# Three edits to the order of work in a fused attention and gated-MLP kernel: joined attention insertions, one accumulator bank for two products, and weight sums at seven in five steps

## The chip, the cores and the metric

The kernel runs on one core of a Trainium2 chip. The metric is the device time of one execution in microseconds (us). PE is the matmul engine (TensorE), DVE the vector engine, ACT the scalar engine, POOL the GpSimd engine, and SP issues the DMAs from one queue, in order.

## The reference

```python
scores = scale * np.matmul(q_c, k_c.transpose(0, 1, 2, 4, 3))      # chunks of 64 tokens, head_dim 64, 64 heads in all
attn = softmax(scores)                                             # over the 64 keys of the chunk
x = (attn @ v_c)  -> (4608 tokens, 512)
gate = 1.0 / (1.0 + np.exp(-(x @ w_gate)))                         # w_gate, w_val: 512 x 1536
out = gate * (x @ w_val) @ w_out                                   # w_out: 1536 x 512
```

Everything is float32; the MLP products are made of three products of float32r halves (high x high, low x high, high x low).

## The kernel before

The 4608 tokens are nine blocks of 512 (`m` = 0 to 8), the hidden layer is twelve tiles of 128 (`f`). Attention is cut into 36 units, four to a block; a unit is one `products` (scores, L163, eight small matmuls), a softmax on DVE and ACT, a turn of the probabilities on DVE (`spread`, L554, sixteen 32x32-block transposes), and one `values` (product with v, L224, eight small matmuls, whose result ACT copies out of PSUM).

Blocks 0 to 2 are done plainly: a step `hidden` (L267) makes one hidden tile with 24 matmuls of 128x512 and `down` (L281) adds it to four output accumulators with 12. Blocks 3 to 8 are done as three pairs (`n` = 0 to 2). In a pair, an item is two hidden tiles of one weight (`p` of six, `which` = gate or value; 12 items), and its four 512-token results come from seven products instead of eight (a Strassen-Winograd scheme); each `product` (L416) is six matmuls of 128x512. The operands that the scheme needs are sums of weight quarters and of x quarters. Products are numbered 1 to 7. Product 1 accumulates in bank `x`, 6 in `y`, 2 on top of 1 in `x`, 7 and 4 on top in `y`, 5 in a third bank `z` (`sole`, L426), 3 on top in `z`. DVE reads `y` and `z` between them: u2 after 6 (L439), u3 after 7 (L458), c22 after 5 (L460), c21 after 4 (L475), c12 after 3 (L478). Per item `i` the program runs `first(i)` (products 1, 6), `last(i-1)` (4, 3) and `middle(i)` (5, 7, 2). Bank `z` alternates between `g0` and `g1`, by `which`. After the items a pair runs 24 `outward` steps (L494), the second weight matrix.

The attention of later blocks is woven in by a generator, `flow` (L506). It yields small DVE costs that `tick` (L573) releases by a credit (`SHARES`, L45), and two letters for PE work that `insert` (L587) releases at set places: "S" for the scores of two units, "A" for the values of two units. In the pairs the two letters come at different places. PE and DVE keep the program's order here; `manual_schedule` says so.

The weight sums are made once, on POOL, while blocks 1 and 2 run: `keep(2)` (L661) asks for two of 24 `keep_sums` (L331) after each step from block 1, `f` = 2. One `keep_sums` is two adds into `a_val`, four into `a_sum`, a cast and a subtract into `a_both`, and one DMA to DRAM. `a_val` and `a_sum` share the two-buffer ring `ob` with the output tiles of `evacuate` (L294, PSUM copy at L305 or L307, DMA at L308); `a_both` has one buffer. `load_group` (L360) loads given weights and sums again for each item.

Of the kernel before, what the change touches and what calls it, by code (L numbers as in the profile page):

```python
# [8 lines left out]
F32 = mybir.dt.float32  # L9
# [3 lines left out]
ALU = mybir.AluOpType  # L13
AX = mybir.AxisListType

P = 128
D = 64
NB = 9
TB = 512
# [22 lines left out]
FIRST_PAIR = 3  # L42


SHARES = {1: 2.5, 2: 2.8, "up": 1.05, "down": 1.3}  # L45


@with_exitstack
def chunk_attn_moe(ctx: ExitStack, tc: tile.TileContext, q, k, v, w, out):


    nc = tc.nc
# [7 lines left out]
    ps_g = ctx.enter_context(tc.tile_pool(name="ps_g", bufs=2, space=bass.MemoryType.PSUM))  # L60
# [94 lines left out]
    def load_values(j):  # L155
        m, h, u = units[j]
        vt = ap2.tile([P, 2, 4, D], F32, name="vt")
        nc.sync.dma_start(vt, v[2 * m + h, u].rearrange("p (a c d) -> p a c d", a=2, c=4))
        state[j]["vt"] = vt

    def products(j):  # L163
        s = state[j]
        sc = ps_a.tile([P, 512], F32, tag="psa", name="sc")
        for a in range(2):
            for t in range(2):
                for c in ((0, 1), (1, 0))[a * t]:
                    n0 = (2 * t + c) * D
                    nc.tensor.matmul(  # L170
                        sc[c * D:(c + 1) * D, (2 * a + t) * P:(2 * a + t + 1) * P],
                        lhsT=s["qt"][:, a, n0:n0 + D], rhs=s["kb"][:, a, :, n0:n0 + D],
                        start=True, stop=True,
                    )
        return sc.rearrange("p (g k) -> p g k", k=D)
# [182 lines left out]
    groups, wo, xc, hid = {}, {}, {}, {}  # L358
# [55 lines left out]
    banks = {}  # L414

    def product(n, p, which, r, bank, start, stop):  # L416
        lhs, name = groups[n, p, which][r]
        x, k = xc[n, name], 0
        for c in range(2):
            for wpart, part in ((0, 0), (0, 1), (1, 0)):  # L420
                nc.tensor.matmul(  # L421
                    bank, lhsT=lhs(wpart, c), rhs=x[:, part, c], start=start and k == 0, stop=stop and k == 5,
                    skip_group_check=True)
                k += 1

    def sole(n, p, which):  # L426
        z = ps_g.tile([P, TB], F32, tag=f"g{which}", name="cz", bufs=1)
        product(n, p, which, 5, z, True, True)
        return z

# [11 lines left out]
    def gated(n, f, b, value):  # L442

        h = hid[n, f][:, b]
        nc.vector.tensor_tensor(out=h, in0=value, in1=h, op=ALU.mult)

    def middle(n, p, which):
        x, y, s1, u2 = banks[n, p, which]
        f = 2 * p
        if which == 0:  # L450
            for i in range(2):
                hid[n, f + i] = wp.tile([P, 2, TB], F32, tag=f"o{f + i}", name="hid")
        z = banks.pop((n, "z"), None) or sole(n, p, which)
        if (p, which) == (0, 0):
            product(n, p, which, 2, x, False, True)
        product(n, p, which, 7, y, False, True)
        u3 = mp.tile([P, TB], F32, tag="ob", name="u3")
        nc.vector.tensor_tensor(out=u3, in0=y, in1=s1, op=ALU.add)  # L458
        c22 = hid[n, f + 1][:, 1] if which == 0 else u3
        nc.vector.tensor_tensor(out=c22, in0=z, in1=u3, op=ALU.add)  # L460
        if (p, which) != (0, 0):
            product(n, p, which, 2, x, False, True)
        if which == 0:
            nc.scalar.activation(hid[n, f][:, 0], x, AF.Sigmoid)
        else:
            gated(n, f + 1, 1, u3)
            gated(n, f, 0, x)
        banks[n, p, which] = y, z, s1, u2

    def last(n, p, which):  # L470
        y, z, s1, u2 = banks.pop((n, p, which))
        f = 2 * p
        product(n, p, which, 4, y, False, True)
        c21 = hid[n, f + 1][:, 0] if which == 0 else s1
        nc.vector.tensor_tensor(out=c21, in0=y, in1=s1, op=ALU.add)  # L475
        product(n, p, which, 3, z, False, True)
        c12 = hid[n, f][:, 1] if which == 0 else u2
        nc.vector.tensor_tensor(out=c12, in0=z, in1=u2, op=ALU.add)  # L478
        if which == 0:
            nc.scalar.activation(hid[n, f + 1], hid[n, f + 1], AF.Sigmoid)  # L480
            nc.scalar.activation(hid[n, f][:, 1], hid[n, f][:, 1], AF.Sigmoid)
        else:
            gated(n, f + 1, 0, s1)
            gated(n, f, 1, u2)

    def split(n, f, b):
        h = hid[n, f][:, b]
# [18 lines left out]
    def flow():  # L506


        kept = None
        for j in range(8, 4 * NB + 2, 2):  # L510
            more = j < 4 * NB
            if more:
                yield "S"
                scv = [products(j), products(j + 1)]
                if j + 2 < 4 * NB:
                    load(j + 2), load(j + 3)
                if kept:
                    yield from spread(*kept, range(12, 16))
                pr = ap2.tile([P, 2, 8, D], F32, name="pr", bufs=1)
                for i in range(2):  # L520
                    yield 1.4
                    mx = sm.tile([P, 8], F32, name="mx")
                    nc.vector.reduce_max(out=mx, in_=scv[i], axis=AX.X)
                    nc.vector.tensor_tensor(
                        out=pr[:, i], in0=scv[i], in1=mx.unsqueeze(2).broadcast_to([P, 8, D]), op=ALU.subtract)
                pr = pr.rearrange("p u g k -> p (u g) k")
                nc.scalar.activation(pr, pr, AF.Exp, scale=0.125)
            elif kept:
                yield from spread(*kept, range(12, 16))
            if kept:  # L530
                yield "A"
                values(j - 2), values(j - 1)
                if more:
                    load_values(j), load_values(j + 1)
            else:
                yield "wait"
            n, rest = divmod(j - 4 * FIRST_PAIR, 8)
            if n > 0 and rest == 0:
                yield ("open", n - 1)
                yield from operands(n - 1)  # L540
            if not more:
                return
            yield 1.5
            sums = sm.tile([P, 16], F32, name="sums2", bufs=1)
            nc.vector.reduce_sum(out=sums, in_=pr, axis=AX.X)
            nc.vector.tensor_scalar_add(out=sums, in0=sums, scalar1=1e-9)
            inv = sm.tile([P, 16], F32, name="inv2", bufs=1)
            nc.vector.reciprocal(out=inv, in_=sums)
            yield 1.2
            nc.vector.tensor_tensor(out=pr, in0=pr, in1=inv.unsqueeze(2).broadcast_to([P, 16, D]), op=ALU.mult)  # L550
            kept = pr, pbd2
            yield from spread(*kept, range(12))
# [10 lines left out]
            nc.vector.transpose(out=pb[dst, :, c, h, i, :], in_=ps[src, h::2, k, :])  # L563

    ahead = flow()
    now = dict(item=next(ahead), credit=0.0, ticks=0, since=0, unit=8, open=-1)

    def advance():
        now["unit"] += 2 * (now["item"] == "A")
        now["item"] = next(ahead, None)  # L570
        now["since"] = now["ticks"]

# [14 lines left out]
    def insert(upto=4 * NB, pieces=0):  # L587


        if now["item"] == "S" or (  # L590
                now["item"] == "A" and now["unit"] < upto and now["ticks"] >= now["since"] + pieces):
            advance()

    def due(n):
# [39 lines left out]
        run(op)  # L634
    kept = [(p, which, c) for p in range(6) for which in range(2) for c in range(2)]

    def keep(n):
        for _ in range(n):
            if kept:
                p, which, c = kept.pop(0)  # L640
                if c == 0:
                    keep_given(p, which)
                keep_sums(p, which, c)

    def rest():
        for m in range(1, FIRST_PAIR):
            upto = 4 * (m + 2) if m == 1 else 4 * (m + 3)
            for f in range(2 if m == 1 else 0, NF):
                if m == 2 and f == 7:
                    now["open"] = 0  # L650
                step(m, f, "")
                tick(SHARES[m])
                insert(upto, 2)
                finish()
                tick(SHARES[m])
                insert(upto, 2)
                if m == 1:
                    keep_outer(f)
                    if f == 11:
                        keep_outer(0), keep_outer(1)  # L660
                keep(2)  # L661
                if m == 2:
                    if f == 8:
                        for which in range(2):
                            load_group(0, 0, which)
        for n in range(3):
            m0 = FIRST_PAIR + 2 * n
            upto = 4 * (m0 + 4)
            order = [(p, which) for p in range(6) for which in range(2)]
            due(n)  # L670
            for i, (p, which) in enumerate(order):
# [77 lines left out]
```

## Time and profile before

| | us |
|---|---|
| median of 3 runs (lowest, highest) | 956.03 (954.69, 957.15) |
| the profiled execution: its time | 960.18 |
| the profiled execution: its span | 958.4 |
| PE busy in that span | 929.6 (97%) |
| DVE, ACT, POOL busy | 601.8, 340.7, 134.1 |

PE is busy almost throughout, so what counts is where it is not, where it runs at the lower clock, and how many matmuls of which length it must issue. Idle time of the other engines costs nothing by itself. The span is from the first to the last instruction of one execution.

### The profile page before, as it was taken

The page shows a single profiled execution, that of the slowest core. Times are in us where ns is not written, and L with a number is a line of the kernel's source. Part 1 is how long each engine was busy: PE and PEld are TensorE (multiplying, and loading weights), DVE is VectorE, ACT ScalarE, POOL GpSimd, SP SyncE. Part 2 cuts the span into 40 slices and gives each one's busy share as a digit, 9 for nine tenths or more (in the row PEclk, how much of TensorE's full clock was granted, in tenths as well). Part 3 has the DMA queues.
Part 4 walks back from the last instruction along what each step waited for, and adds up shares of the span by engine and source line. Part 5 has one row for each costly group of instructions (what it writes and reads, how often), then busy time and mean ns, then how long its engine had stood idle before and what let it go on. Part 6 is the DMA issues. An engine that isn't in the chain of part 4 may idle for free.

```text
span 958.4 us, 13077 instructions
## 1 busy us (share of the span) xinstructions
PE 929.6 (97%) x4960; PEld 763.5 (80%) x4960; DVE 601.8 (63%) x999; ACT 340.7 (36%) x556; POOL 134.1 (14%) x204
## 2 busy tenths in 40 slices
PE   6999999999969999999999999999999999999998
PEld 4777888888847888788888888888888888888886
DVE  6889973676527657777677675677776635544432
ACT  5799752233214323231333432313143321112222
POOL 1000006999838000000000000000000000000000
PEclk7999999999989999999999999999999999999999
DMA  8688985444453343657666756666565655556661
GB/s 270 215 287 299 307 309 180 132 133 129 136 164 109 102 132 132 193 198 226 207 212 239 252 198 218 228 202 206 179 231 191 218 211 192 196 188 209 220 220 44
DMA packets 81279, 189.61 MB, mean 198 GB/s; under 512 B 7488, under 2 KB 38208, under 8 KB 76608
## 3 DMA queue, kind: packets, MB, share of 16 engines
q1 hardware_dynamic: 81216, 188.77, 58.9%
q8 instruction: 39, 0.64, 0.3%
q14 instruction: 24, 0.20, 0.1%
HBM read 150.99 MB, written 37.75 MB: 197 GB/s over the span
## 4 chain that ended last, share of the span: by engine, by line
PE 70%; POOL 9%; DMA 8%; DVE 5%; ACT 4%; issue 2%; SPq 1%; ACTq 0%; DVEq 0%; POOLq 0%
PE acc L499 21%; PE cy L421 15%; PE cz L421 10%; PE cx L421 10%; PE g L261 6%; PE acc L287 4%; DMA w_raw<-w_in 3%; POOL a_sum L344 3%; POOL a_both L347 3%; DMA sums<-a_both 2%; POOL a_val L338 2%; PE sc L170 2%; PE av L231 2%; POOL a_both L346 1%; DMA out<-ob 1%
## 5 line engine op out<-in xcount | busy, mean ns | idle before, releaser
L261 PE MATMUL g<-xt,w 128*128 128x512 f32 (+1 forms) x960 | 208.7, 372 | 6.0 <-ACT hf L270 1.7
L261 PEld LDWEIGHTS g<-xt,w 128*128 128x128 f32 x960 | 168.1, 189 | 41.5 <-ACT hf L270 4.0
L499 PE MATMUL acc<-wr,hh 128*128 128x512 f32 x576 | 177.7, 390 | 0.0
L421 PE MATMUL cy<-xc,wr 128*128 128x512 f32 x648 | 159.4, 389 | 0.4 <-DVE u L458 0.4
L421 PEld LDWEIGHTS cy<-xc,wr 128*128 128x128 f32 x648 | 121.6, 188 | 26.0 <-DVE u L458 0.8
L499 PEld LDWEIGHTS acc<-wr,hh 128*128 128x128 f32 x576 | 107.9, 188 | 22.7 <-ACT raw L242 0.3
L499 PE MATMUL acc<-wr,hl 128*128 128x512 f32 x288 | 112.0, 389 | 0.0
L421 PE MATMUL cz<-xc,wr 128*128 128x512 f32 x432 | 106.3, 391 | 0.0
L421 PE MATMUL cx<-xc,wr 128*128 128x512 f32 x432 | 106.2, 391 | 0.0
L563 DVE STREAM_TRANSPOSE pbd<-pr 32x256 f32<-32x256 f32 x224 | 97.7, 436 | 4.1
L491 DVE TENSOR_TENSOR hl<-hid,hh 128x512 fp32r<-128x512 f32 x72 | 49.6, 688 | 79.0 <-ACT hh L489 75.8
L421 PEld LDWEIGHTS cz<-xc,wr 128*128 128x128 f32 x432 | 80.6, 188 | 17.6 <-issue 1.2
L421 PEld LDWEIGHTS cx<-xc,wr 128*128 128x128 f32 x432 | 80.7, 188 | 17.4 <-issue 0.9
L287 PE MATMUL acc<-w,hh 128*128 128x512 f32 x288 | 90.6, 396 | 1.1 <-ACT hh L274 0.7
L489 ACT CAST hh<-hid 128x512 fp32r<-128x512 f32 x72 | 44.8, 623 | 123.7 <-PE acc L499 96.3
L287 PEld LDWEIGHTS acc<-w,hh 128*128 128x128 f32 x288 | 52.6, 188 | 13.8 <-issue 1.9
L499 PEld LDWEIGHTS acc<-wr,hl 128*128 128x128 f32 x288 | 54.1, 188 | 11.3
L272 DVE TENSOR_TENSOR hf<-g,hf 128x512 f32<-128x512 f32 (+1 forms) x40 | 25.4, 635 | 57.8 <-PE g L261 53.8
L439 DVE TENSOR_TENSOR u<-cy,s 128x512 f32<-128x512 f32 x36 | 24.8, 688 | 57.9 <-PE cy L421 57.8
L338 POOL TENSOR_TENSOR a_val<-w 128x256 f32<-128x256 f32 x48 | 37.7, 805 | 163.8 <-ACT xt L249 147.4
L458 DVE TENSOR_TENSOR u<-cy,s 128x512 f32<-128x512 f32 x36 | 24.9, 690 | 53.9 <-PE cy L421 53.8
L287 PE MATMUL acc<-w,hl 128*128 128x512 f32 x144 | 56.1, 390 | 0.0
(103 smaller groups left out, 1006.5 us busy)
## 6 DMA issues: line engine op xcount, KB each, us to landing
wr<-sums SPq DMA_DIRECT2D x72, 512.0 KB, 4.5
wr<-outer SPq DMA_DIRECT2D x36, 1024.0 KB, 4.8
w_raw<-w_in SPq DMA_DIRECT2D x36, 512.0 KB, 5.8
wr<-given SPq DMA_DIRECT2D x36, 512.0 KB, 3.6
sums<-a_both SPq DMA_DIRECT2D x24, 512.0 KB, 3.5
qt<-q_in SPq DMA_DIRECT2D x36, 256.0 KB, 4.4
kbd<-k_in SPq DMA_DIRECT2D x72, 128.0 KB, 4.4
vt<-v_in SPq DMA_DIRECT2D x36, 256.0 KB, 4.1
```

Source lines behind the costliest of these rows:

```text
L261: nc.tensor.matmul(ps[:, tok], lhsT=wt[f, which][:, wpart, c:c + P], rhs=x[:, part, i, tok], start=n == 0, stop=n == 11)
L272: nc.vector.tensor_tensor(out=hf, in0=pv, in1=hf, op=ALU.mult)
L287: nc.tensor.matmul(acc[m, t], lhsT=hx[:, ts], rhs=wt[f, 2][:, wpart], start=f == 0 and i == 0, stop=f == NF - 1 and i == 2,)
L338: nc.gpsimd.tensor_tensor(out=val[:, 2 * n:2 * n + 2], in0=parts[:, 0], in1=parts[:, 1], op=ALU.add)
L344: nc.gpsimd.tensor_tensor(out=o, in0=x, in1=y, op=op)
L347: nc.gpsimd.tensor_tensor(out=both[:, :, 1], in0=sm4, in1=both[:, :, 0].bitcast(F32), op=ALU.subtract)
L421: nc.tensor.matmul(bank, lhsT=lhs(wpart, c), rhs=x[:, part, c], start=start and k == 0, stop=stop and k == 5, skip_group_check=True)
L458: nc.vector.tensor_tensor(out=u3, in0=y, in1=s1, op=ALU.add)
L489: nc.scalar.copy(hh, h)
L491: nc.vector.tensor_tensor(out=hl, in0=h, in1=hh.bitcast(F32), op=ALU.subtract)
L499: nc.tensor.matmul(acc[m, t], lhsT=hx[:, ts], rhs=wo[f][:, wpart], start=f == 0 and i == 0, stop=f == NF - 1 and i == 2)
L563: nc.vector.transpose(out=pb[dst, :, c, h, i, :], in_=ps[src, h::2, k, :])
```

## The change

Four edits. (1) In the pairs, "A" and "S" become one letter "AS": the values of two units and then the scores of the next two are issued back to back. The first of these scores goes into bank `g1`, the second into the shared `psa` ring of two, whose two buffers the two `values` have just filled. All sixteen transposes of a unit pair now stand ahead of the insertion; before, four came after the scores. (2) Bank `z` is always `g0`, and the order inside an item's products is 3, 4 in `last` and 7, 5, 2 in `middle` (the first item of a pair excepted). (3) Credit per tick in the pairs is 1.15, not 1.05. (4) The weight sums are asked for at seven in five steps instead of ten.

```diff
-SHARES = {1: 2.5, 2: 2.8, "up": 1.05, "down": 1.3}
+SHARES = {1: 2.5, 2: 2.8, "up": 1.15, "down": 1.3}
-    def products(j):
+    def products(j, apart=False):
-        sc = ps_a.tile([P, 512], F32, tag="psa", name="sc")
+        sc = ps_g.tile([P, 512], F32, tag="g1", name="sc", bufs=1) if apart else ps_a.tile(
+            [P, 512], F32, tag="psa", name="sc")
     def sole(n, p, which):
-        z = ps_g.tile([P, TB], F32, tag=f"g{which}", name="cz", bufs=1)
+        z = ps_g.tile([P, TB], F32, tag="g0", name="cz", bufs=1)
     def middle(n, p, which):
-        z = banks.pop((n, "z"), None) or sole(n, p, which)
         if (p, which) == (0, 0):
+            z = banks.pop((n, "z"), None) or sole(n, p, which)
             product(n, p, which, 2, x, False, True)
-        product(n, p, which, 7, y, False, True)
+            product(n, p, which, 7, y, False, True)
+        else:
+            product(n, p, which, 7, y, False, True)
+            z = sole(n, p, which)
     def last(n, p, which):
+        product(n, p, which, 3, z, False, True)
+        c12 = hid[n, f][:, 1] if which == 0 else u2
+        nc.vector.tensor_tensor(out=c12, in0=z, in1=u2, op=ALU.add)
         product(n, p, which, 4, y, False, True)
...
-        product(n, p, which, 3, z, False, True)
-        c12 = hid[n, f][:, 1] if which == 0 else u2
-        nc.vector.tensor_tensor(out=c12, in0=z, in1=u2, op=ALU.add)
     def flow():
+            joined = now["joined"]
+            if more and joined:
+                yield from spread(*kept, range(12, 16))
+                yield "AS"
+                values(j - 2), values(j - 1)
+                scv = [products(j, True), products(j + 1)]
+                load_values(j), load_values(j + 1)
+            elif more:
                 yield "S"
                 scv = [products(j), products(j + 1)]
...
-    def keep(n):
-        for _ in range(n):
+    def keep(done, wanted):
+        for _ in range(wanted - done):
...
-                keep(2)
+                keep(24 - len(kept), (7 * (12 * m + f - 13)) // 5)
...
-            upto = 4 * (m0 + 4)
+            upto = 4 * NB
+            now["joined"] = True
```

SP's queue around the output tiles of block 1 (`out<-ob`), before: 20 of the 24 sums stand ahead of the output tiles, the last six of them here.

```order
L348 DMA sums_2428<-a_both 512x1x256 x2
L348 DMA sums_2537<-a_both 512x1x256
L158 DMA vt<-v_in 128x512 x2
L348 DMA sums_2537<-a_both 512x1x256
L348 DMA sums_2627<-a_both 512x1x256 x2
L149 DMA qt<-q_in 128x512
L152 DMA kbd_87<-k_in 64x2x256 x2
L149 DMA qt<-q_in 128x512
L152 DMA kbd_88<-k_in 64x2x256 x2
L158 DMA vt<-v_in 128x512 x2
L308 DMA out<-ob 128x512 x4
```

And now:

```order
L349 DMA sums_2540<-a_both 512x1x256 x2
L149 DMA qt<-q_in 128x512
L152 DMA kbd_87<-k_in 64x2x256 x2
L149 DMA qt<-q_in 128x512
L152 DMA kbd_88<-k_in 64x2x256 x2
L158 DMA vt<-v_in 128x512 x2
L149 DMA qt<-q_in 128x512
L152 DMA kbd_87<-k_in 64x2x256 x2
L149 DMA qt<-q_in 128x512
L152 DMA kbd_88<-k_in 64x2x256 x2
L158 DMA vt<-v_in 128x512 x2
L309 DMA out<-ob 128x512 x4
```

Fourteen sums now stand ahead of the output tiles and ten behind them; between the fourteenth and the output tiles SP has two sets of loads of q, k and v and no sum.

PE in the first pair, items 2 and 3 (operands: `xc_3454` is product 1's, 3504 is 6's, 3520 4's, 3463 3's, 3460 5's, 3467 7's, 3456 2's; all weights `wr`), before:

```order
L421 MATMUL cx_3822<-xc_3454,wr_3743 128x512 x6
L421 MATMUL cy_3823<-xc_3504,wr_3743 128x512 x6
L421 MATMUL cy_3750<-xc_3520,wr_3647 128x512 x6
L421 MATMUL cz_3790<-xc_3463,wr_3647 128x512 x6
L231 MATMUL av_3860<-pbd_89,vt_3438 64x128 x8
L231 MATMUL av_3871<-pbd_89,vt_3440 64x128 x8
L421 MATMUL cz_3886<-xc_3460,wr_3743 128x512 x6
L421 MATMUL cy_3823<-xc_3467,wr_3744 128x512 x6
L421 MATMUL cx_3822<-xc_3456,wr_3743 128x512 x6
```

And now, items 1 and 2:

```order
L422 MATMUL cx_3724<-xc_3454,wr_3646 128x512 x6
L422 MATMUL cy_3725<-xc_3504,wr_3646 128x512 x6
L422 MATMUL cz_3698<-xc_3463,wr_3380 128x512 x6
L422 MATMUL cy_3653<-xc_3520,wr_3380 128x512 x6
L232 MATMUL av_3761<-pbd_89,vt_3438 64x128 x8
L232 MATMUL av_3772<-pbd_89,vt_3440 64x128 x8
L171 MATMUL sc_3783<-kbd0_87,qt_3284 64x128 x8
L171 MATMUL sc_3792<-kbd1_88,qt_3288 64x128 x8
L422 MATMUL cy_3725<-xc_3467,wr_3647 128x512 x6
L422 MATMUL cz_3822<-xc_3460,wr_3646 128x512 x6
L422 MATMUL cx_3724<-xc_3456,wr_3646 128x512 x6
```

Product 3 moved ahead of 4 and product 5 behind 7, so products 4 and 7 stand between the two users of `z`; the scores, which before stood at other places in the program, now follow the values directly. Over the three pairs, seven insertions of scores and eight of values become seven joined ones and one of values.

## Rows read from the trace of the kernel before

**Rows 1.** Waits of PE in the whole span: us in total, times, longest us.

```profile
PE sc L170 <- DMA kbd<-k_in: 10.8, 4, 8.1
```

**Rows 2.** Windows, by stage: us, busy us of each engine, PE clock, DMA share, GB/s.

```profile
263.00:300.00 37.00, 26.04 (x125) 19.96 (x124) 16.31 (x29) 5.61 (x8) 19.47 (x29) 0.91 0.46 142
```

**Rows 3.** Timeline of PE, 258 to 300 us (start us, us, what, [idle before]).

```profile
263.49 5.60 PE L261 MATMUL g<-xt,w 128*128 128x512 f32 x24
277.19 1.97 PE L170 MATMUL sc<-kbd,qt 128*64 128x128 f32 x16 [8.10 <-DMA kbd<-k_in]
292.95 0.62 PE L287 MATMUL acc<-w,hh 128*128 128x512 f32 x2
```

**Rows 4.** Timeline of SP's queue, 258 to 284 us.

```profile
258.30 12.81 SPq L348 DMA_DIRECT2D sums<-a_both  x3
271.83 1.65 SPq L152 DMA_DIRECT2D kbd<-k_in  x2
276.53 7.59 SPq L308 DMA_DIRECT2D out<-ob  x4
```

**Rows 5.** Timeline of DVE and ACT, 255 to 300 us: output tiles of block 1.

```profile
267.25 0.69 DVE L307 COPY ob<-acc 128x512 f32<-128x512 f32 x1 [5.70 <-POOL a_sum L344]
270.60 0.58 ACT L305 COPY ob<-acc 128x512 f32<-128x512 f32 x1 [9.25 <-POOL a_both L347]
282.55 0.69 DVE L307 COPY ob<-acc 128x512 f32<-128x512 f32 x1 [14.62 <-DMA out<-ob]
```

**Rows 6.** Timeline of POOL: first, fourteenth and twentieth weight sum.

```profile
152.05 1.45 POOL L338 TENSOR_TENSOR a_val<-w 128x256 f32<-128x256 f32 x2 [147.36 <-ACT xt L249]
233.75 1.29 POOL L347 TENSOR_TENSOR a_both<-a_sum,a_both 128x512 fp32r<-128x512 f32 x1
269.31 1.26 POOL L347 TENSOR_TENSOR a_both<-a_sum,a_both 128x512 fp32r<-128x512 f32 x1
```

**Rows 7.** Chain that ended last, 143 to 156 us: output tiles of block 0.

```profile
146.47 3.23 DMA out<-ob
```

**Rows 8.** Timeline of PE around one insertion, first pair, 440 to 447 us.

```profile
440.80 1.52 PE L421 MATMUL cx<-xc,wr 128*128 128x512 f32 x6
442.25 1.97 PE L170 MATMUL sc<-kbd,qt 128*64 128x128 f32 x32
444.15 1.65 PE L421 MATMUL cx<-xc,wr 128*128 128x512 f32 x6
445.64 1.52 PE L421 MATMUL cy<-xc,wr 128*128 128x512 f32 x6
```

**Rows 9.** Timeline of PE and DVE, 389 to 396 us: the first pair's first items.

```profile
391.00 1.52 PE L421 MATMUL cy<-xc,wr 128*128 128x512 f32 x6
392.91 1.65 PE L421 MATMUL cy<-xc,wr 128*128 128x512 f32 x6 [0.39 <-DVE u L458]
392.89 0.69 DVE L460 TENSOR_TENSOR hid<-cz,u 128x512 f32<-128x512 f32 x1
```

**Rows 10.** Timeline of PE and ACT: values and the copies of them.

```profile
459.33 1.97 PE L231 MATMUL av<-pbd,vt 128*64 128x128 f32 x32
462.69 0.57 ACT L242 COPY raw<-av 128x512 f32<-128x512 f32 x1
546.48 0.58 ACT L242 COPY raw<-av 128x512 f32<-128x512 f32 x1 [0.16 <-PE av L231]
```

**Rows 11.** Timeline of PE and DVE, 616 to 630 us: a round with DVE behind.

```profile
620.96 2.88 PE L421 MATMUL cy<-xc,wr 128*128 128x512 f32 x12
623.68 2.88 PE L421 MATMUL cz<-xc,wr 128*128 128x512 f32 x12
625.59 0.66 DVE L478 TENSOR_TENSOR u<-cz,u 128x512 f32<-128x512 f32 x1
```

**Rows 12.** Windows, DVE's hl (L276) alone: beside POOL's sums, and after them.

```profile
155.00:255.00 100.00, 10.64 (x12) 1.00 0.40 126
310.00:378.00 68.00, 4.84 (x7) 1.00 0.39 120
```

More of the change, by code (lines that the diff above doesn't have):

```diff
@@ L482, in last @@
         else:
+            gated(n, f, 1, u2)
             gated(n, f + 1, 0, s1)
-            gated(n, f, 1, u2)
     def split(n, f, b):
@@ L511, in flow @@
             more = j < 4 * NB
-            if more:
+            joined = now["joined"]
[6 more added lines that the diff above has]
+            elif more:
                 yield "S"
                 scv = [products(j), products(j + 1)]
+            if more:
                 if j + 2 < 4 * NB:
                     load(j + 2), load(j + 3)
-                if kept:
+                if kept and not joined:
                     yield from spread(*kept, range(12, 16))
@@ L529, in flow @@
                 yield from spread(*kept, range(12, 16))
-            if kept:
+            if kept and not (more and joined):
                 yield "A"
@@ L565, in chunk_attn_moe @@
     ahead = flow()
-    now = dict(item=next(ahead), credit=0.0, ticks=0, since=0, unit=8, open=-1)
+    now = dict(credit=0.0, ticks=0, since=0, unit=8, open=-1, joined=False)
+    now["item"] = next(ahead)
     def advance():
-        now["unit"] += 2 * (now["item"] == "A")
+        now["unit"] += 2 * (now["item"] in ("A", "AS"))
         now["item"] = next(ahead, None)
@@ L590, in insert @@
         if now["item"] == "S" or (
-                now["item"] == "A" and now["unit"] < upto and now["ticks"] >= now["since"] + pieces):
+                now["item"] in ("A", "AS") and now["unit"] < upto and now["ticks"] >= now["since"] + pieces):
             advance()
```

## Prediction

> **What bounds the kernel now.** I read the table of busy times first: PE is busy for 97% of the span, so a change can win only where PE is idle or slow, or where it issues less. PE's waits then name the one large idle stretch: of all that PE waits for, the keys of a score matmul cost most, 10.8 us, of which one wait is 8.1 us [rows 1]. The windows by stage show where: in the 37 us from 263 to 300, PE is busy for 26.04 and its granted clock is 0.91 of full [rows 2]; in the stretches of the pairs it is never idle by more than a few tenths. So the third block's start is one target, and the number and the spacing of small insertions in the pairs is the other.
>
> How much the stall costs is read from PE's own order. Six matmuls of 128x512 take 1.36 us (twelve from 620.96 to 623.68) [rows 11]. An insertion of two units costs 445.64 - 440.80 - 2 x 1.36 = 2.12 us all in, of which the 32 records of its small matmuls take 1.90 and the way in and out 0.22 [rows 8]. From 263.49 PE has 24 matmuls of the up kind (5.44), one insertion of scores (2.12), twelve down (2.72) and 24 up (5.44), and should begin the next down block at 279.21. It begins it at 292.95 [rows 3]. So **13.74 us** are lost, 10.96 as idle time [rows 2], the rest because PE runs at half rate after the long wait: 16 records of scores take the 1.97 us there that 32 take elsewhere [rows 3, 8].
>
> Who causes it is read on SP and POOL. The keys that PE waits for are issued at 271.83, because SP, in order, sat on three weight sums from 258.30 for 12.81 us [rows 4]. POOL makes the first sum from 152.05 and ends the twentieth at 270.57: 5.93 us each [rows 6]. Twenty of them are asked for ahead of block 1's output tiles, in less time than POOL needs. The output copies use the same ring as the sums, so DVE's waits for POOL until 267.25 and ACT's until 270.60; the third copy, DVE's second, waits until 282.55 for an output DMA that SP could issue only at 276.53 [rows 4, 5], and what stands behind it on DVE is late too.
>
> **The change part by part.**
>
> *Weight sums, seven in five steps.* Fourteen now stand ahead of block 1's output tiles. POOL ended its fourteenth at 235.04 [rows 6], 28 us before the tiles are due at 263.5. Copies one and two then find a free ring, SP has no sum to sit on, and the keys are loaded long before 269. The 13.74 us go. What is late next is the third copy: it needs the first output DMA, issued at about 262.5, which lands 3.23 us later by block 0's row [rows 7], or 6.0 by block 1's (276.53 to 282.55) [rows 4, 5], so at 265.7 to 268.5. Its accumulator is wanted again at 263.49 + 5.44 + 2.12 + 1.36 = 272.4, so the DMA is covered; some DVE work queues behind the copy. I give back **0.3** and bound that by 0 and 3 us, half of one slow DMA. The other ten sums move beside the third block: 10 x 5.93 = 59 us of POOL from about 270 to 330, when that block ends at about 366. There SP again meets sums ahead of loads of q, k and v; I take 0, since these loads are asked for some 10 us or more ahead of their use, and bound it by a repeat of the 8.1 us wait [rows 1]. POOL's adds slow DVE: twelve `hl` took 0.887 us each beside the sums, seven took 0.691 after them [rows 12]. That is 0.2 us for each of some four more steps, on an engine off the path.
>
> *Joined insertions.* No matmul goes or comes. Seven pairs of stops become seven stops, so seven ways in and out of 0.22 us go: **1.54**. The seam between values and scores is taken as nothing, since two units follow each other inside 32 records without one; its bounds are 0 and a full 0.22, that is 0 to 1.54 in all. The second score goes into the bank of the first values, so it waits for ACT's copy of them. It is due three quarters into the insertion, 3 x 0.95 = 2.85 us after its start. Where ACT was free the copy began 0.16 us after the ACT work before it, as soon as the values were done, and took 0.58 [rows 10]: done at about 1.8. Where ACT stood behind a softmax and two sigmoids it ended at 463.26, 3.93 us after the values began at 459.33 [rows 10]: 1.08 late. In the new order ACT's instruction ahead of these copies is the copy of the next item's product 1, finished long before. I take 0 and bound it by 7 x 1.08 = 7.6.
>
> *Order 3, 4, 7, 5, 2 with one bank z.* Product 5 now overwrites the bank that DVE reads after product 3. Between them stand 4 and 7. Counted from the start of 3, it ends at 1.36, its last matmul drains by 1.52 [rows 8], DVE can add at about 1.63 and is done 0.69 later, at 2.32; product 5 is due at 3 x 1.36 = 4.08. That leaves 1.7 us for DVE to be late. In a round with DVE well behind, 3 began at 623.68 and its add at 625.59, 1.91 after it, so 0.28 late [rows 11]. So 33 rounds cost nothing. One place does cost: in the first pair DVE has a softmax between the sums, and 4, which waits only for u3, began at 392.91 instead of 391.00 + 1.36 [rows 9]. Now 3 comes first and waits for c22, done at 393.58: **0.7** more, once. The other two pairs have no softmax there. Here the Trainium skill's page Perfetto Trace Analysis (Optimizing Tensor Performance, Matmuls) speaks against the change: independent groups should rotate through PSUM banks, so that one's evacuation overlaps the next one's matmuls. By that rule every round would show its evacuation; by the row above it does not, because two products to another bank stand between.
>
> *More credit per tick* moves DVE's softmax pieces earlier and adds no work; PE covers it as before. Loads of v, q and k are now issued together at the joined stop, a round or more ahead of use; I take 0.
>
> Sum: -13.74 + 0.30 - 1.54 + 0.70 = -14.28. The profiled execution took 960.18, so its like would take 945.9. That execution is 4.15 above the median of the runs; taken from the median, **941.8**. A difference of 0.3% (2.9 us) is about what a measurement of this kernel can tell from none.
>
> **The rivals.**
> A. The stall moves. POOL restarts behind the output DMAs and SP sits on sums 15 to 24 until a load of keys or values is late in the third block. For it: SP's order has these loads behind sums. Against: POOL's pace leaves some 10 us. It gives back 8.1: 949.9.
> B. A residue at the output tiles, by DVE work queued behind the third copy, or because the profiled execution had a worse stall than the others (it is 4.15 slower than their median): 3 to 4 us back, 945 to 946.
> C. The second score waits for ACT in each joined stop: 7.6 back, 949.4. Against: ACT's order there.
> D. **Slower**: the single bank z. If DVE ends its add of 3 after product 5 is due, PE stops in 33 rounds. The gain is used up when each loses 14.28 / 33 = 0.43 us, that is when DVE begins the add 1.7 + 0.43 = 2.1 us late in every round; with no overlap at all, 0.27 + 0.69 = 0.96 per round, 32 us, 973.5. For it: DVE is the busiest engine after PE and gets its pieces in bigger lumps. Against: the worst lateness that I found is 0.28.
> The rotation rule of the Trainium skill named above is this rival's mechanism; the trace so far does not bear it out.
> E. Sums still late: the change would not do what it says if POOL were held by something else than its own pace. POOL's sums follow each other without gaps up to the twentieth, which speaks against; little would change, 955.
>
> **How the numbers follow.** Forecast 0.72, A 0.07, B 0.13, C 0.04, D 0.03, E 0.01. Faster by over 0.3%: all but D and E, 0.96; within 0.3%: 0.01; slower: 0.03. The range reaches down to the sum without the give-backs less the runs' own scatter of 1.3 (956.03 - 13.74 - 1.54 - 1.3 = 939.4, so 939.5), and up over B to 948.0.
>
> **What would show it.** In the profile after: PE's long wait for keys is gone, and the windows of the third block show PE full and a granted clock of 1.0; POOL's sums show a gap at block 1's output tiles after the fourteenth and end at about 330; output copies of block 1 wait for PE or one DMA, not for POOL. In the pairs 64 small records stand together seven times, with one way in and out of 0.22. Product 5 does not wait for DVE's c12; the first pair's product 3 waits about 1.2 us for c22. It is wrong if PE waits at product 5, at the second score of a joined stop, or for keys, values or `hl` in the third block.

## The result and the profile after

The changed kernel takes **945.29 us** (median of 5 runs, 944.48 to 945.75); the kernel before takes 956.03 (5 runs beside it, 954.69 to 958.22). The ratio is 0.9883, 95% interval 0.9867 to 0.9900: about 11 us faster. I had said 941.8 with a range of 939.5 to 948.0. The profiled execution of the changed kernel took 945.75, its span is 944.0; before, these were 960.18 and 958.4. So the profiled executions differ by 14.4 and the medians by 10.7; 960.18 lies above all five runs of the kernel before.

The page of the changed kernel, busy times and the slices of PE, POOL and PE's granted clock:

```profile
PE 926.0 (98%) x4960; PEld 763.6 (81%) x4960; DVE 602.9 (64%) x999; ACT 342.5 (36%) x556; POOL 134.1 (14%) x204
PE   6999999999999999999999999999999999999998
POOL 1000005997069700000000000000000000000000
PEclk7999999999999999999999999999999999999999
```

The single low slice in the middle of POOL's row is the pause that the new pacing makes at block 1's output tiles. Three of PE's waits over the span, where [rows 1] stood before (us in total, times, longest):

```profile
PE sc L171 <- DMA kbd<-k_in: 1.3, 2, 1.1
PE cz L422 <- DVE hid L464: 1.1, 1, 1.1
PE acc L503 <- ACT ob L306: 0.6, 1, 0.6
```

The wait of 8.1 for keys is gone (the 1.3 that are left belong to the start). Two small waits in the pairs are new. The window that answers to [rows 2] (us, busy us of PE, PEld, DVE, ACT, POOL, PE clock, DMA share, GB/s):

```profile
262.00:300.00 38.00, 38.00 (x237) 31.15 (x236) 26.34 (x45) 13.74 (x18) 30.17 (x43) 1.00 0.39 131
```

PE is never idle there and runs at full clock, where it was busy for 26.04 of 37 before. The timeline of the same stretch, all engines (start us, us, what, [idle before]), against [rows 3 to 6]:

```profile
232.58 1.30 POOL L348 TENSOR_TENSOR a_both<-a_sum,a_both 128x512 fp32r<-128x512 f32 x1
...
261.74 4.21 SPq L309 DMA_DIRECT2D out<-ob  x4
...
262.82 5.60 PE L262 MATMUL g<-xt,w 128*128 128x512 f32 x24
...
264.26 0.69 DVE L308 COPY ob<-acc 128x512 f32<-128x512 f32 x1 [2.54 <-DMA out<-ob]
...
267.16 1.97 POOL L339 TENSOR_TENSOR a_val<-w 128x256 f32<-128x256 f32 x2 [33.28 <-DMA out<-ob]
...
268.35 1.97 PE L171 MATMUL sc<-kbd,qt 128*64 128x128 f32 x32
...
278.54 0.62 PE L288 MATMUL acc<-w,hh 128*128 128x512 f32 x2
```

POOL ends its fourteenth sum at 233.88 and waits until the output tiles have left. The output DMAs go at 261.74, not 276.53; the third copy waits for one of them and is done at 264.95, 6.8 us before PE wants that bank. From the 24 matmuls to the second down block PE needs 278.54 - 262.82 = 15.72, which is what its matmuls add up to without a stall; before it needed 29.46 [rows 3].

### The profile page after: what moved, and what is told of

Its sections match the earlier page's. It is cut to its first block, busy times and chain, and to the rows that moved or that the text cites. A ratio compares the mean times of both kernels' runs of the same rounds, so it can differ in the third digit from the quotient of the medians.

```text
span 944.0 us, 13066 instructions
## 1 busy us (share of the span) xinstructions
PE 926.0 (98%) x4960; PEld 763.6 (81%) x4960; DVE 602.9 (64%) x999; ACT 342.5 (36%) x556; POOL 134.1 (14%) x204
## 4 chain that ended last, share of the span: by engine, by line
PE 83%; DVE 6%; DMA 5%; ACT 4%; issue 1%; SPq 1%; ACTq 0%; DVEq 0%
PE acc L503 20%; PE cy L422 15%; PE g L262 14%; PE cz L422 10%; PE cx L422 10%; PE acc L288 7%; DMA w_raw<-w_in 4%; PE av L232 3%; PE sc L171 3%; DVE w_raw L132 1%; DVE w L137 1%; DVE w_raw L134 1%; ACT w_raw L130 1%; DMA wr<-outer 1%; ACT w_raw L129 1%
## 5 line engine op out<-in xcount | busy, mean ns | idle before, releaser
L422 PE MATMUL cz<-xc,wr 128*128 128x512 f32 x432 | 109.8, 389 | 1.1 <-DVE hid L464 1.1
L440 DVE TENSOR_TENSOR u<-cy,s 128x512 f32<-128x512 f32 x36 | 24.9, 691 | 54.2 <-PE cy L422 54.1
L468 ACT ACTIVATE hid<-cx 128x512 f32<-128x512 f32 x18 | 10.8, 599 | 108.2 <-PE cx L422 108.2
```

The source lines that it names most:

```text
L422: nc.tensor.matmul(bank, lhsT=lhs(wpart, c), rhs=x[:, part, c], start=start and k == 0, stop=stop and k == 5, skip_group_check=True)
L440: nc.vector.tensor_tensor(out=u2, in0=y, in1=s1, op=ALU.add)
```

## Where PE's time went, in three stretches

All profiled executions were cut in the same way. A is the start of the 24 up matmuls after block 1's last down block (263.49 in [rows 3]); B is the time from there to the first pair's first product; C is the time from that product to the start of the last outward matmul. For the changed kernel B and C rest on these two rows of PE's timeline (365.30 - 262.82 = 102.48, 939.23 - 365.30 = 573.93):

```profile
365.30 1.52 PE L422 MATMUL cz<-xc,wr 128*128 128x512 f32 x6
...
939.23 0.39 PE L503 MATMUL acc<-wr,hl 128*128 128x512 f32 x1
```

| profiled execution of | A | B | C | span |
|---|---|---|---|---|
| before | 263.49 | 116.63 | 573.53 | 958.4 |
| before, another (e12) | 259.08 | 115.19 | 573.53 | 952.5 |
| changed | 262.82 | 102.48 | 573.93 | 944.0 |
| changed, another (e5) | 262.52 | 102.48 | 573.98 | 943.7 |
| e1 before + new pacing | 263.78 | 102.48 | 573.54 | 944.1 |
| e7 before + nine in five | 263.05 | 102.80 | 573.53 | 944.1 |
| e2 changed, old pacing | 262.45 | 116.14 | 573.92 | 957.4 |
| e6 before, keys from ACT | 276.00 | 102.48 | 573.53 | 956.7 |
| e3 changed, s1 first | 259.66 | 102.48 | 572.65 | 939.5 |
| e4 changed, three mends | 260.79 | 102.48 | 571.65 | 939.6 |
| e8 changed, not joined | 262.15 | 102.48 | 575.77 | 944.7 |
| e10 one product between | 260.56 | 102.48 | 579.83 | 947.6 |
| e9 5 directly behind 3 | 263.11 | 102.48 | 606.26 | 976.6 |
| e11 e4 with a fuller start | 263.45 | 102.48 | 571.63 | 942.3 |

Three things are seen at once. B is 102.48 wherever the sums are paced (102.80 in e7), and 12.7 to 14.2 more where they are not: that is the stall, and it is not the same in each execution. (In e6 the stall stands ahead of A, so A holds it.) C repeats to 0.06 where the program in it is the same, so a few tenths in the pairs can be read from one execution: the pairs became **0.40 longer**, not 0.84 shorter as my terms for them sum to. And the start, A, scatters by 4.7 us (e6 aside) between executions whose program up to there is the same or nearly so; that scatter is in the times of the runs.

## The experiments

**e1 and e2: pacing alone, and all the rest alone.** e1 is the kernel before with `keep(24 - len(kept), (7 * (12 * m + f - 13)) // 5)`; e2 is the changed kernel with

```diff
-                keep(24 - len(kept), (7 * (12 * m + f - 13)) // 5)
+                keep(24 - len(kept), 2 * (12 * m + f - 13))
```

> The kernel before with the weight sums at seven in five steps, nothing else. Theory: the pacing alone removes the stall at block 1's output tiles, and the edits in the pairs come to about nothing together (seven joined stops save 0.37 each, 2.6 in all; given back are 0.71 at the first pair's first item, 3 x 0.46 at the second outward step of each pair and 0.84 at an output tile of the first pair), net +0.3. Then this run takes 945.0, 0.3 below the changed kernel. Rival 1: the pairs gain 0.84, as the prediction's terms for them sum to; then 946.1. Rival 2: the stall cost all executions 13.74, as in the profiled one, and the pairs lose 3; then 942.3. In the trace: no wait for keys at 268, and the pairs as before.

> The changed kernel with the old pacing of the weight sums, two after each step. Theory: the stall is back, its size from one execution to the next as in the kernel before, and the median is 956.4 (before + 0.3). Rival 1 (the pairs gain 0.84): 955.2. Rival 2 (the pairs lose 3): 959. In the trace: a wait for keys of several us near 268 to 277 and copies of output tiles that wait for POOL.

e1: 944.52 against 957.92 before, ratio 0.9871 (0.9850 to 0.9892). e2: 957.99, ratio 1.0005 (0.9988 to 1.0021). So the pacing carries the whole gain, and the edits in the pairs together give nothing that the times show. The times cannot tell e1 from the changed kernel (0.9883); the stretches can: C is 573.54 and 573.92, the same 0.4 apart as between before and changed.

**e7: how few sums ahead are few enough.** Before with `9 *` in place of `7 *`.

> The kernel before with the sums at nine in five steps: 18 ahead of block 1's output tiles instead of 20 (the change: 14). Theory: what counts is that POOL is through with those ahead when the tiles are due. The eighteenth ends at 152.05 + 18 x 5.93 = 258.8, before 263.5, so the stall is gone and the time is that of seven in five (12 to 13 below the kernel before), within 2. Rival: the stall falls with the number of sums ahead (two of six fewer, a third); then some 9 of 13.7 stay.

945.44, ratio 0.9873 (0.9841 to 0.9904); B is 102.80, the stall is gone but for 0.32. Timeline of e7, POOL and SP:

```profile
256.49 1.29 POOL L347 TENSOR_TENSOR a_both<-a_sum,a_both 128x512 fp32r<-128x512 f32 x1
...
259.05 1.59 SPq L152 DMA_DIRECT2D kbd<-k_in  x2
...
264.07 5.77 SPq L308 DMA_DIRECT2D out<-ob  x4
...
271.23 1.93 POOL L338 TENSOR_TENSOR a_val<-w 128x256 f32<-128x256 f32 x2 [13.45 <-DMA out<-ob]
```

The eighteenth sum ends at 257.78, five us ahead of the 24 matmuls at 263.05. With two sums more, in the kernel before, POOL ends the twentieth at 270.57 [rows 6], seven us after the same matmuls have begun, and all of the stall is there. So the stall does not fall in step with the number of sums; it fits POOL being through in time or not.

**e6: the keys by another queue.** In the kernel before, `nc.scalar.dma_start` for the keys of units 16 and 17.

> The kernel before, with the keys of units 16 and 17 (the ones that PE waits 8.1 for) loaded from ACT's queue instead of SP's; everything else, the pacing too, as before. Theory: the late keys are one of two effects of the same cause; the scores then start on time, but the output copies still wait for POOL and SP until 282.55, so the down step that needs their banks (due at 279.2 without a stall) and hf behind them stay late: about 8 of 13.7 come back, 948 where the kernel before takes 956. Rival 1: the keys alone are the stall; then 13.7 come back, as with the new pacing. Rival 2: the output copies alone set it; then under 2 come back.

956.36, ratio 0.9980 (0.9958 to 1.0003). This does not tell what it was meant to tell. The stall moved: ACT, timeline of e6, stood at these loads for 17 us, and PE waited 9.55 for ACT's sigmoid, one step ahead of where it waits in the kernel before (A is 276.00, B 102.48):

```profile
244.70 17.38 ACTq L152 DMA_DIRECT2D kbd<-k_in  x4
262.19 0.60 ACT L270 ACTIVATE hf<-g 128x512 f32<-128x512 f32 x1 [20.45 <-DMA sums<-a_both]
```

The profile names a sum's DMA as what let ACT go, and the records of the trace show why. A DMA reports its landing by a semaphore (a counter that the next instruction waits for), and this program has eight of them for all its DMAs, taken in turn by both queues. In all 460 cases where a semaphore is used again, the DMA is issued only after the one before it with that semaphore has landed. The second load of keys in e6 has the semaphore of the sum issued at 252.52, which landed at 256.01; the load goes at 256.03. The fourth has that of the sum issued at 258.04. Chain that ended last, e6 (start us, us, what):

```profile
252.52 3.49 DMA sums<-a_both
...
258.04 3.43 DMA sums<-a_both
...
261.55 0.54 ACTq L152
```

So the loads left SP's queue and were held by the sums all the same. My text said that the keys were late because SP issues in order; for the kernel before the trace bears that out (the third sum of [rows 4] goes at 270.59, 0.02 after POOL has made it, and the keys next), and e6 does not speak against it.

How the 13.7 divide between late keys and late copies can be read in the kernel before. Its chain that ended last runs from POOL over SP to the third output copy and DVE's work behind it, and not through the scores:

```profile
269.31 1.27 POOL a_both L347
...
270.59 0.51 SPq L348
...
276.53 5.90 DMA out<-ob
...
282.55 0.69 DVE ob L307
...
289.31 0.70 DVE hf L272
```

PE's own timeline agrees:

```profile
283.30 0.73 PE L287 MATMUL acc<-w,hh 128*128 128x512 f32 x2 [0.35 <-DVE ob L307]
```

This is the third accumulator, due at 272.4 without a stall. With the keys in time PE would have stood there until 283.3 all the same. So the longest wait on PE's list, 8.1 for the keys, hides behind the copies, and bringing the keys alone forward should give back next to nothing. That is worked out from these rows; no run shows it.

**e12: the kernel before once more.**

> The kernel before, unchanged, for another profiled execution. Theory: the stall at block 1's output tiles is the same 13.7 in each execution, the pairs take 573.5, and what scatters is the start (up to 35 us). Rival (B of the prediction): the stall itself is 3 to 4 smaller in executions that are nearer to the median.

955.93, ratio 1.0001 (0.9989 to 1.0013). Its span is 5.9 below that of the execution the prediction was made from: 4.41 of it in A, 1.44 in B. Timeline of e12:

```profile
272.04 6.21 SPq L308 DMA_DIRECT2D out<-ob  x4
...
276.70 0.69 DVE L307 COPY ob<-acc 128x512 f32<-128x512 f32 x1 [13.26 <-DMA out<-ob]
```

The third copy starts 4.66 after the first output DMA's issue here and 6.0 in the execution before [rows 4, 5], and so much earlier does the stall end. Both the theory (the start scatters) and the rival (the stall does) are half right; B exceeds 102.48 by 14.15, 13.66 and 12.71 in three executions. The second of these is e2, whose third copy stands here:

```profile
280.98 0.69 DVE L308 COPY ob<-acc 128x512 f32<-128x512 f32 x1 [14.06 <-DMA out<-ob]
```

From the start of this copy to the first pair's first product all three take the same: 97.57 (before), 97.61 (e2), 97.57 (e12). From the start of the late scores (277.19, 275.55, 271.69) they take 102.93, 103.04 and 102.58. So the size of the stall goes with the copy and not with the keys.

**e5 and e8: joined and not joined.** e5 is the changed kernel again. e8 takes out one line:

```diff
-            now["joined"] = True
```

> The changed kernel again, as the control of the runs beside it. Its profiled execution began with PE at half rate from 21 to 27 us, which two other kernels with the same program up to there did not have (they stood 2 to 3 us earlier at 35 us). Theory: that is scatter between executions; from the first pair's first product to the last matmul this execution takes 573.9 again, whatever its start. Rival: the pairs vary too, by more than 0.3.

> The changed kernel with the values and the next scores inserted apart again, everything else (order of products, one bank z, credit, pacing) as changed. Theory: the seven joined stops save 0.37 each, 2.6 in all, and in the pairs' span by the trace that comes back: 573.9 becomes 576.5, less up to 0.84 if the output tile of the first pair is no longer late. Rival (my prediction's term): 1.54, so 575.4. If joining were what makes the single bank z possible, PE would also wait at products 5 or 3.

e5: 946.21, ratio 0.9882 (0.9855 to 0.9909); its C, 573.98, repeats the first execution's 573.93, so the pairs do not vary. e8: 946.54, ratio 0.9890 (0.9864 to 0.9916). The runs can't tell them apart; C can: 575.77 against 573.98, and in e8 PE does not wait at the first pair's output tile. 573.93 + 2.59 - 0.84 = 575.68, as the theory had it. One joined stop of the changed kernel, PE and ACT:

```profile
389.82 1.52 PE L422 MATMUL cy<-xc,wr 128*128 128x512 f32 x6
391.27 1.97 PE L232 MATMUL av<-pbd,vt 128*64 128x128 f32 x32
392.42 0.59 ACT L243 COPY raw<-av 128x512 f32<-128x512 f32 x1 [4.48 <-PE av L232]
393.07 1.92 PE L171 MATMUL sc<-kbd,qt 128*64 128x128 f32 x32
394.92 1.65 PE L422 MATMUL cy<-xc,wr 128*128 128x512 f32 x6
396.41 1.52 PE L422 MATMUL cz<-xc,wr 128*128 128x512 f32 x6
```

It costs 396.41 - 389.82 - 2 x 1.36 = 3.87 all in, so 0.37 less than two single ones (4.24): 0.22 for the way in and out, and 0.15 because the 64 records take 3.65 together where 2 x 32 take 3.80. ACT has copied the first values at 393.01, a microsecond before the second score is due.

**e9 and e10: the bank z with less between.** e9 has order 4, 3, 5, 7, 2 and e10 has 3, 4, 5, 7, 2. In `middle` both have

```diff
-            product(n, p, which, 7, y, False, True)
             z = sole(n, p, which)
+            product(n, p, which, 7, y, False, True)
```

and e9 also has product 4 with its sum ahead of 3 in `last`.

> The changed kernel with products 4 and 7 no longer between 3 and 5: order 4, 3, 5, 7, 2, one bank z. Dose of my rival D. In the changed kernel's trace DVE has ended c12 1.83 us before product 5 starts in 18 of the 33 rounds, and 1.0 to 1.8 in nine more (six have an insertion between). Theory: with both products gone (2.72) PE waits for DVE at product 5 in all rounds without an insertion, 0.89 each at least, 26 to 30 in all; the pairs take 600 to 604 instead of 573.9, the kernel about 972. Rival: some of it is hidden (the adds come earlier as well); then under 15.

> Half that dose: order 3, 4, 5, 7, 2, one bank z, so that only product 4 stands between 3 and 5. Theory: the spare time of 1.83 falls by 1.36 to 0.47, so 18 rounds still lose nothing; the six with 1.0 to lose 0.3 each and the first pair's first round 0.8: 2 to 3 in all, the pairs take 576 to 577, the kernel 948. Rival: the bank costs nothing as long as any product stands between (573.9); or lateness adds up (over 580).

e9: 976.95, ratio 1.0216 (1.0193 to 1.0239), C + 32.3. e10: 950.11, ratio 0.9939 (0.9918 to 0.9959), C + 5.9. Timeline of e9, one round, PE and DVE:

```profile
843.76 1.52 PE L422 MATMUL cz<-xc,wr 128*128 128x512 f32 x6
845.32 0.69 DVE L482 TENSOR_TENSOR u<-cz,u 128x512 f32<-128x512 f32 x1 [0.67 <-PE cz L422]
846.06 1.66 PE L422 MATMUL cz<-xc,wr 128*128 128x512 f32 x6 [0.78 <-DVE u L482]
```

The second `cz` is 0.94 later than 843.76 + 1.36. This happens in 26 rounds, with some 0.13 lost in the matmuls behind each wait, and once with 2.16. So my rival D had its price right (0.96 a round, 32 us, 973.5) and its condition not met: in the changed kernel DVE's c12 ends 1.83 us before product 5 in 17 of 33 rounds (not 18, as I had counted), and more than 0.5 in every other. One such round, PE and DVE:

```profile
599.56 2.88 PE L422 MATMUL cy<-xc,wr 128*128 128x512 f32 x12
...
599.76 0.69 DVE L479 TENSOR_TENSOR hid<-cz,u 128x512 f32<-128x512 f32 x1 [0.60 <-PE cz L422]
...
602.28 1.52 PE L422 MATMUL cz<-xc,wr 128*128 128x512 f32 x6
```

The Trainium skill's rule on rotating banks (Perfetto Trace Analysis, Optimizing Tensor Performance, Matmuls) holds where nothing stands between the two users of a bank, as e9 shows with 0.94 a round; with two products to another bank between them the trace shows no such cost. e10 lost twice what I expected: in a round where PE waits 0.20 it loses 0.37 up to the next product and 0.12 more in that product, and c22, which now waits for 7, made product 3 late in three rounds.

**e3 and e4: the losses that I had not seen.** PE makes two stops at the second outward step of each pair, too short for the list of waits. Timeline of the changed kernel, DVE, ACT and PE:

```profile
496.67 0.69 DVE L446 TENSOR_TENSOR hid<-s,hid 128x512 f32<-128x512 f32 x1
...
497.39 1.24 ACT L493 CAST hh<-hid 128x512 fp32r<-128x512 f32 x2 [3.60 <-DVE hid L446]
...
498.06 0.73 PE L503 MATMUL acc<-wr,hh 128*128 128x512 f32 x2
498.79 0.50 PE L503 MATMUL acc<-wr,hl 128*128 128x512 f32 x1
```

`hh` shares a ring of two with `s1` (tag `hh`, L436 and L492). The change also put the gate product that reads s1 last (two lines that the diff above leaves out), so the cast of `hh` starts 0.68 later, and PE loses 0.46 in each of three pairs. e3 swaps the two back:

```diff
-            gated(n, f, 1, u2)
             gated(n, f + 1, 0, s1)
+            gated(n, f, 1, u2)
```

> The changed kernel with the two gate products at the end of an item in the old order (the one that reads s1 first). Theory: PE's two short stops at the second outward step of each pair (0.46 each) come from the ring that s1 shares with hh: the cast of hh waits for the gate product that reads s1, and this product now stands last. Swapped back, it ends 0.6 earlier, hh and hl are there in time, and the time falls by 3 x 0.46 = 1.4 to 943.9. Rival: the stops come from DVE's lateness after product 4 as such; then the time stays at 945.3 and the stops remain.

942.04, ratio 0.9845 (0.9820 to 0.9870). C falls by 1.28 to 572.65 and the stops are gone; that the time falls by more goes with an earlier start, as far as the profiled execution shows (A is 259.66), and not with the swap. The second loss, changed kernel, ACT and PE:

```profile
532.76 1.04 ACT L403 CAST xc<-raw 128x1024 fp32r<-128x1024 f32 x1
533.71 0.57 ACT L306 COPY ob<-acc 128x512 f32<-128x512 f32 x1
534.34 0.73 PE L503 MATMUL acc<-wr,hh 128*128 128x512 f32 x2 [0.56 <-ACT ob L306]
```

The first pair's last joined stop comes behind the ninth of twelve outward steps of a block, where the values came behind the twelfth before, so the casts of the next pair's operands now stand on ACT ahead of an output copy; PE loses 0.84 there. e4 has e3's swap and two mends more: product 4 ahead of 3 in the first pair's first item, and for the first pair `now["open"] = n + 1` only when `b` is 1.

> The changed kernel with three mends: the gate products swapped back (1.4), the first item of the first pair with product 4 ahead of 3 again (0.7), and the casts of the second pair's operands held until the first pair's first output tiles are copied (0.84). Theory: the three losses add, 945.3 - 2.9 = 942.4, and in the trace PE has no wait in the pairs. Rival: they hide one another or come back elsewhere (the operands late for the second pair, c12 late for product 5); then 943.9 or more.

941.42 (941.15 to 945.28), ratio 0.9847 (0.9822 to 0.9873), the lowest of all medians, but the ratio is that of e3 (0.9845): the times can't tell the two apart. C falls by 2.28, not 2.93: the first pair's round still loses time, 0.38 of it in a wait for u3 as before the change [rows 9], and its product 5 starts 0.25 late for DVE. So the mends add up to four fifths.

**e11: the start.** e4 with eight more matmuls into `sink`, six behind the second scores and two behind the first turn.

> The changed kernel with the three mends, and eight more matmuls in the first 15 us, six behind the second scores and two behind the first turn, where PE else waits for DVE (their result is not used). Theory: the start scatters by 2 to 3 us from one execution to the next because PE's granted clock is at half for a longer or shorter stretch between 10 and 27 us, after PE has waited; with the gap filled the clock stays up, PE stands at 35 us where the faster executions stood or ahead of it, and the times scatter less: median 939 to 941, spread under 2. Rival: the start waits for DVE, ACT and the loads at either clock, and only the extra matmuls show: 941 to 943, spread as before.

943.98 (941.46 to 945.20), ratio 0.9871 (0.9850 to 0.9892). A miss: no better than e4, A is 263.45. The granted clock was 0.92 from 10 to 15 us, where e4 had 0.79, but fell to 0.76 and 0.81 in the two stretches from 19 to 27.

## Why the prediction was right, and where not

- *What bounds it, and the stall (-13.74).* Right. PE's 13.74 are gone to the hundredth in the changed kernel and e1 and, but for 0.3, in e7, and the stall is back in e2. That POOL's pace is the cause is shown by e1, e2 and e7; that the shared ring carries it is read from the copies' waits [rows 5] and the chain, and no run changes the ring. Of the two effects that I named, late keys and late copies, the copies set the time (e6, e12). The third block lost another 0.41 after the stall that I had not counted, which went with it.
- *Residue (+0.30).* None: the output DMA landed in time, at the bound of 0.
- *POOL's other sums.* They run beside the third block and end at 328.63, as predicted; no load was late (rival A fell). Seven `hl` took 8.15 in all beside them, 1.16 each, four took 2.77 after them, 0.69 each, and PE waited for none. The Trainium skill (SBUF — State Buffer, Who interferes with whom) says that a DVE instruction with two SBUF inputs and a GpSimd one that reads SBUF exclude each other; the longer time beside the sums agrees.
- *Joined stops (-1.54).* Mechanism right, size off: 7 x 0.37 = 2.59. I priced the way in and out and not the records, which take 0.15 less in one piece. The second score never waited 7.6 (rival C fell).
- *First pair (+0.70).* Right: the round that lost 0.68 before loses 1.40, 0.72 more; PE waits 1.10 for c22, where I had said about 1.2.
- *Order 3, 4, 7, 5, 2, "33 rounds cost nothing".* Right for bank z (e9, e10). Wrong for what else moved with the order: I followed the bank and not the two gate products behind it, 3 x 0.46. The other loss, 0.84, belongs to the joined stops: they bring the last values of the first pair from behind the twelfth outward step to behind the ninth, and the next pair's operands with them. I had no term for it. It is not the credit, which I took at 0: e8 has the same credit, its values stand behind the twelfth step, and the loss is gone (whether joining alone, at the old credit, brings it, no run shows). My terms for the pairs sum to -0.84; measured -2.59 + 0.72 + 1.38 + 0.84 = +0.35, by C +0.40.
- *From the median, 941.8.* The step that failed most. The sum -14.28 stands beside -14.4 between the two profiled executions, and 945.9 from the execution's own time is 0.6 above the median measured. In part that is luck: -0.67 of the -14.4 is start, and without it the executions differ by 13.75, where 1.24 lost on the terms of the pairs is set off by the 0.41 that I had not counted and the 0.30 that I gave back for nothing. I took the sum from the median instead, as if the stall were the same in each execution. It was largest in the one that I read: 14.15 in B, against 13.66 and 12.71 in two others. That is the second half of rival B, which I gave 0.13, and the measured 945.29 is B's time (945 to 946), not the forecast's; but the other two stalls are 0.5 and 1.4 smaller, and B wanted 3 to 4. How much of 956.03 - 945.29 is stall and how much is start can't be said from times alone.

## What to carry to other kernels

Ask for background work no faster than its engine does it when it shares a ring or a queue with results that are due: eighteen sums ahead cost 0.3 us here, and two more the whole stall. The longest wait on a list need not be the one that sets the time: follow the chain that ended last, and see which wait the size of the loss goes with. When products change places, follow every buffer that their results share a ring with, down to the last reader, for a reader that moves 0.7 us can stop another engine. Cut a profile at the same instructions in each execution and compare stretch by stretch: a few tenths show there that runs with 3 us of scatter hide; and take a sum from the time of the execution that it was read from.

## What was not expected of the hardware

The start scatters with PE's granted clock. From 19 to 27 us, the changed kernel and e3, whose programs differ only far later (columns as in [rows 2]):

```profile
19.00:27.00 8.00, 7.00 (x43) 5.70 (x44) 5.37 (x11) 3.71 (x7) 0.00 (x0) 0.58 0.87 309
```

```profile
19.00:27.00 8.00, 6.41 (x56) 4.95 (x56) 7.66 (x16) 6.54 (x24) 0.00 (x0) 0.98 0.91 298
```

At a granted clock of 0.58 PE does 43 matmuls in these 8 us, mostly at 1.2 GHz; at 0.98 it does 56, nearly all at 2.4 GHz. The first down block starts at 33.01 and 30.05. Over all fourteen profiled executions the clock of this stretch is 0.50 to 0.58 in five, 0.79 in six (e11 with its extra matmuls among them) and 0.96 to 1.00 in three, and the first down block starts at 32.4 to 33.4, 31.3 to 33.0 and 29.9 to 30.9. That is not all of A's scatter: from there to A the executions take 227.7 to 231.2 (e6 aside). In the two executions shown PE had been idle for up to 2.9 us at a time before. What decides which start an execution gets was not found (e11).
